# When and where the first expert's weights are split into high and low parts

## The chip, the cores and the metric

The kernel runs on one core of a Trainium2 chip. The metric is the device time of one execution in microseconds (us), as the median of several runs. Five engines work at once, each through its own queue in the order of the program: TensorE (PE, matrix products; its weight loads show as PEld), VectorE (DVE), ScalarE (ACT), GpSimd (POOL) and SyncE (SP), which issues most transfers. ScalarE and GpSimd issue some too.

## The reference

Three stages follow one another, on 4 x 448 = 1792 tokens of width 768:

```python
scores = scale * q @ k.T                 # 4 batches, 12 heads, 448 x 448
scores = einsum('bhij,hg->bgij', scores, w_pre)
attn = softmax(scores)
attn = einsum('bhij,hg->bgij', attn, w_post)
x = attn @ v                             # as 1792 x 768
...
expert_idx = argmax(normalised(x) @ normalised(expert_emb).T / tau)
out[mask] = gate[mask] * (relu(x[mask] @ w1[e]) @ w2[e])   # 8 experts, 768 -> 1024 -> 768
...
h = x @ w_in                             # 768 -> 2048 -> 768
g = h - tanh(h)
return g @ w_out
```

## The kernel before

**Precision.** Weights and activations come as 32-bit floats, and a product is made of three products of rounded parts: high times high, high times low, low times high. A weight tile is therefore split in two steps: a copy that rounds to the high part, and a subtraction of the high part from the tile, which gives the low part. `split1` (L633) does both: the copy by `cpy` (ScalarE unless told otherwise, L637), the subtraction by `eng` (VectorE unless told otherwise, L639).

**Attention.** The score rows are cut into blocks of ten rows times twelve heads. The loop at L1013 goes over the steps s; in step s the block s is multiplied by `w_pre` on TensorE (`emit_P`, tile `P`), VectorE takes its row maximum, and ScalarE its exponential with the row sum (L374). In the next step VectorE makes the scaled weights `w` from `wpost` and the row sums (`emit_W`, L384). Two steps after its start the block is multiplied by `w` on TensorE (`T_mm`, tile `T`, L406) and ScalarE copies the result to `A` (L411). Side work has a position in the table `side`: `at(pos, fn, ...)` puts a call into step pos. `emit_AV` multiplies `A` by v, `emit_X` transposes that to token rows, writes them to `x_d` in memory and makes the routing logits, and `emit_R` assigns tokens to experts, in five parts.

**The way to the experts.** `to_experts` in step NBK - 7 opens the buffers of the expert stage and requests four tiles of w1 and four of w2 (`feed1`, `feed2`). The weights w1 of an expert are six tiles of 128 x 1024 (chunks c = 0 to 5, 512 KB each). The list `q1` holds all w1 tiles of all experts in order, and each `feed1` requests the next one into a ring of four buffers (`r1`, NB1 = 4); SyncE waits until the buffer's last reader, a subtraction, is through. `do1` splits one tile and then, unless `feed=False`, calls `feed1`. So the number of tiles that are requested and not yet split stays what it is when the first expert starts. Four `do1` calls of expert 0 stand in the steps NBK - 5 to NBK - 2, with the copy on VectorE and the subtraction on GpSimd. After the loop come the chunks 4 and 5 (copy on ScalarE, subtraction on GpSimd, no `feed1`), the last token tiles (`emit_AV`, `emit_X`, `emit_R` with copies on VectorE), the gathers of expert 0's token rows by GpSimd, their transposition (`xsplit`, L654, tiles `xti`, `xhi`, `xli`), and two `feed1` on ScalarE's queue.

**The experts.** For each of eight experts and one overflow item, `h_chunk` makes eight hidden chunks on TensorE (the h phase) while w2 is split by `do2`; some of the chunks also carry a `conv_step`, which loads a piece of a dense weight (`craw`, L107) and stores its conversion (L121). Then `y_half` makes four halves of the output (the y phase), and a list `todo` is interleaved with them: six `do1` for the next expert, three after the first half and three after the second, then its four `xsplit`. The results are copied from PSUM (tile `yi`) by VectorE for the first half of a pair (L675) and by ScalarE for the second (L673). PSUM tiles of `y_half` and `xsplit` share a ring of five buffers.

Of the kernel before, what the change touches and what calls it, by code (L numbers as in the profile page):

```python
# [8 lines left out]
F32 = mybir.dt.float32  # L9
F32R = mybir.dt.float32r  # L10
# [20 lines left out]
def body(ctx: ExitStack, tc, q, k, v, w_pre, w_post, emb, tau, w1, w2, win, wout, out):  # L31
    nc = tc.nc
    pe, act, dve, pool, sp = nc.tensor, nc.scalar, nc.vector, nc.gpsimd, nc.sync
# [3 lines left out]
    E, _, FF = w1.shape  # L37
# [3 lines left out]
    KD = DM // 128  # L41
# [83 lines left out]
    if True:  # L125
# [209 lines left out]
        for T in range(4 * B):  # L335
            n = IT[T % 4][1]
# [6 lines left out]
        NBK = len(blocks)  # L343
# [19 lines left out]
        def emit_P(i):  # L363
            n = 12 * blocks[i][2]
            t = sr.pop(i)
            pt = ps("b", f"P{i}")
            pe.matmul(pt[:n, :S], wpre[:n, :n], t[:n, :], start=True, stop=True)  # L367

            flush2()
            mx = a2.tile([120, 4], F32, tag="mx", name=f"mx{i}", bufs=5)  # L370
            dve.tensor_reduce(mx[:n, 0:1], pt[:n, :S], op=ALU.max, axis=AX.X, negate=True)  # L371
            p = a2.tile([120, S], F32, tag="p", name=f"p{i}", bufs=LAG + 1)
            pj[i] = (p, mx)
            return lambda: act.activation(p[:n, :], pt[:n, :S], AF.Exp, bias=mx[:n, 0:1], scale=1.0, accum_out=mx[:n, 1:2])  # L374
# [3 lines left out]
        def emit_W(i):  # L378
            n = 12 * blocks[i][2]
            p, mx = pj[i]  # L380
            dve.tensor_scalar_add(mx[:n, 2:3], mx[:n, 1:2], 1e-9)  # L381
            dve.reciprocal(mx[:n, 3:4], mx[:n, 2:3])
            w = a2.tile([120, 120], F32, tag="w", name=f"w{i}", bufs=3)
            dve.tensor_scalar_mul(w[:n, :], wpost[:n, :], mx[:n, 3:4])  # L384
            wj[i] = w
# [4 lines left out]
        def emit_T(i):  # L390
            T, r, m = blocks[i]
            n = 12 * m
            b, it = divmod(T, 4)
            if r == 0:
                A[T] = aA.tile([CP, NJ, H, 120], F32, tag="A", name=f"A{T}", bufs=2)
            p, mx = pj.pop(i)
            w = wj.pop(i)
            wv = w.rearrange("p (g i) -> p g i", i=10)[:n, :, :m]
            pt = ps("c", f"T{i}")
            pv = pt[:CP, :NJ * n].rearrange("p (c g i) -> p c g i", c=NJ, i=m)  # L400
            tev[i] = (pt, pv, p, w, wv, n, m)

        def T_mm(i, c0, c1):
            pt, pv, p, w, wv, n, m = tev[i]
            for c in range(c0, c1):
                pe.matmul(pt[:CP, c * n:(c + 1) * n] if m == 10 else pv[:, c], p[:n, c * CP:(c + 1) * CP], w[:n, :] if m == 10 else wv,  # L406
                          start=True, stop=True)

        def emit_TE(i):
            T, r, m = blocks[i]  # L410
            act.copy(A[T][:, :, :, 10 * r:10 * r + m], tev.pop(i)[1])  # L411
# [202 lines left out]
    with mctx:  # L614
        mp, mq = [None], [None]
# [17 lines left out]
        def split1(t, tag, nm, n, eng=dve, cpy=act.copy):  # L633
            w = t.shape[1]
            pl = mp[0] if tag == "w1" else mq[0]
            hi = pl.tile([128, w], F32R, tag=tag + "h", name=f"{tag}h{nm}", bufs=n)
            cpy(hi, t)  # L637
            lo = pl.tile([128, w], F32R, tag=tag + "l", name=f"{tag}l{nm}", bufs=n)
            eng.tensor_sub(lo, t, hi.bitcast(F32))  # L639
            return hi, lo  # L640

        def gather(idx, nm):
            t = mp[0].tile([128, DM], F32, tag="xg", name=f"xg{nm}", bufs=3)
            pool.indirect_dma_start(out=t, out_offset=None, in_=x_d, in_offset=bass.IndirectOffsetOnAxis(ap=idx, axis=0))
            return t

        def xtile(nm):
            return tuple(mq[0].tile([128, KD, 256], F32R, tag=tg, name=f"{tg}{nm}") for tg in ("xh", "xl"))
# [166 lines left out]
        def src1(e, c):  # L815
            return osrc[0](c) if e == OV else w1[e, c * 128:(c + 1) * 128, :]
# [7 lines left out]
        r1, r2 = {}, {}  # L824

        def feed1(eng=sp):
            if q1:
                n, e, c = q1.pop()
                r1[n, c] = mp[0].tile([128, FF], F32, tag="r1", name=f"r1_{n}_{c}", bufs=NB1)
                eng.dma_start(r1[n, c], src1(e, c))  # L830

        def feed2():
            if q2:
                n, e, f = q2.pop()
                r2[n, f] = mp[0].tile([128, DM], F32, tag="r2", name=f"r2_{n}_{f}", bufs=NB2)
                sp.dma_start(r2[n, f], src2(e, f))

        def do1(n, c, out_, eng=dve, cpy=act.copy, feed=True):
            out_.append(split1(r1.pop((n, c)), "w1", f"i{n}_{c}", KD, eng, cpy))
            if feed:  # L840
                feed1()

        def do2(n, f, out_, eng=dve):
            out_.append(split1(r2.pop((n, f)), "w2", f"i{n}_{f}", KF, eng))
            feed2()

        def gathers(n):
            e = items[n]
            ix = [osrc[2]] if e == OV else [ids[:, 2 * e + j:2 * e + j + 1] for j in range(2)]
            return [gather(i, f"i{n}_{j}") for j, i in enumerate(ix)]  # L850
# [4 lines left out]
        def at(pos, fn, *a):  # L855
            side.setdefault(int(pos), []).append((fn, a))
# [68 lines left out]
        w1c = []  # L925
# [8 lines left out]

        at(NBK - 7, to_experts)
        for c in range(4):
            at(NBK - 5 + c, do1, 0, c, w1c, pool, dve.tensor_copy)

        def relay_to(i):
            while nxt[0] <= min(i, NBK - 1) and blocks[nxt[0]][0] in sdone:  # L940
                emit_relay(nxt[0])
                nxt[0] += 1
# [4 lines left out]
        def flush(tag=None):  # L947
            keep = []
            while late:
                x = late.pop(0)  # L950
                if tag in (None, x[0]):
                    y = x[1]()
                    if x[0] == "e" and callable(y):
                        late2.append((x[0], y))
                else:
                    keep.append(x)
            late.extend(keep)
            if tag:
                flush2(tag)
# [9 lines left out]
        def run_fill(fn, a):  # L969
            tag = "d" if fn is emit_AV2 else "e"  # L970
            if fn is emit_S2:
                flush("d")
                flush("e")
            elif fn is not emit_S:
                flush(tag)
            e = fn(*a)
            if fn in (emit_S, emit_S2):
                e()
                if a[1] + (fn is emit_S2) == NP - 1:
                    sdone.add(a[0])  # L980
            else:
                late.append((tag, e))
# [30 lines left out]
        for s in range(NBK + LAG + 6):  # L1013
            todo = side.get(s, [])
            fill = [x for x in todo if x[0] in PEF]
            for fn, a in todo:
                if fn in (load_q, load_k, load_v, conv_load, zero_fill):
                    fn(*a)
            flush()
            relay_to(s + NSR - 1)  # L1020
            ex = emit_P(s) if s < NBK else lambda: None
            if 0 <= s - 1 < NBK:
                emit_W(s - 1)
            for fn, a in todo:
                if fn is emit_R and a[1] in (0, 1, 3):
                    fn(*a)
            i = s - LAG
            on = 0 <= i < NBK
            fill.sort(key=lambda x: x[0] not in (emit_S, emit_S2, emit_AV2))
            if fill and fill[0][0] in (emit_S, emit_S2, emit_AV2):  # L1030
                run_fill(*fill.pop(0))
            ex()
            for fn, a in todo:
                if fn is conv_do:
                    fn(*a)
            if on:
                emit_T(i)
                T_mm(i, 0, NJ)
                flush("d")
                emit_TE(i)  # L1040
            for x in fill:
                run_fill(*x)
            for fn, a in todo:
                if fn in (to_experts, do1) or fn is emit_R and a[1] in (2, 4):
                    fn(*a)
        flush()
        flush2()
# [2 lines left out]

        ps_late()
        TL = 4 * B - 1
        for c in range(4, KD):
            do1(0, c, w1c, pool, feed=False)
        emit_X(TL - 1, 0)()
        for p in range(3):
            emit_AV(TL, p, dve.tensor_copy)()
# [8 lines left out]
        for x in range(5):  # L1066
            emit_R(len(RG) - 1, x)
        xg = gathers(0)
        xhl = xtile("i0")
        for j, t in enumerate(xg):  # L1070
            for hf in range(2):
# [5 lines left out]
        for n, e in enumerate(items):  # L1077
# [49 lines left out]
            if not last:  # L1127
                w1c, xhl = nw1, nx
# [251 lines left out]
```

## Time and profile before

| What | Before |
|---|---|
| median of 3 runs (lowest to highest) | 1370.86 us (1370.37 to 1372.72) |
| the profiled execution's own time | 1376.32 us |
| its span, first to last instruction | 1374.6 us |
| TensorE busy | 1312.8 us (96%) |
| VectorE busy | 1017.7 us (74%) |
| ScalarE busy | 736.7 us (54%) |
| GpSimd busy | 502.8 us (37%) |
| mean granted TensorE clock | 0.977 of full speed |

The profile shows one execution. All times of the trace count from the span's first instruction. The block loop ends near 518 us, the experts run from 539 to about 845 us, and the dense stage follows. A share of busy time is a mean over stages that differ; what a change in one place is worth is read from the waits of that place.

### The profile page before, as it was taken

The numbers are of one execution on the slowest core, as the hardware profiler recorded it, in microseconds if no ns is written. First come the engines' busy times: TensorE is split into PE (matmuls) and PEld (weight loads), VectorE is DVE, ScalarE is ACT, GpSimd is POOL, SyncE is SP. The second block draws the span as 40 slices with busy tenths as digits, with TensorE's granted clock in tenths as the row PEclk, the third lists the DMA queues.
The fourth block names the chain that finished last, engine by engine and source line by source line (L and its number), as shares of the span: only waits on it lengthen the run. The fifth ranks groups of instructions, "written<-read, shape, count | busy, mean of one in ns | idle before, by whom it ended". The sixth has DMA issues, their size and how long they took to land. (4 is left out here: it accounts for less than half of the span.)

```text
span 1374.6 us, 24956 instructions
## 1 busy us (share of the span) xinstructions
PE 1312.8 (96%) x9104; PEld 1146.0 (83%) x9104; DVE 1017.7 (74%) x2189; ACT 736.7 (54%) x1518; POOL 502.8 (37%) x495
## 2 busy tenths in 40 slices
PE   7999999999999987999999997899999989999998
PEld 5777776776777766999999996699998889999998
DVE  4776787678677773677776764688888788788886
ACT  5666666675666653545444453554444444544441
POOL 0233333333333323333332422544454334444432
PEclk9999999999999997999999999799999999999999
DMA  6886675667556564778877872421113133121102
GB/s 153 247 253 190 185 209 168 170 201 202 160 173 204 164 205 147 263 253 262 273 233 238 254 220 84 136 69 47 46 48 109 37 96 107 67 61 55 47 24 81
DMA packets 149412, 210.90 MB, mean 153 GB/s; under 512 B 54022, under 2 KB 109494, under 8 KB 149286
## 3 DMA queue, kind: packets, MB, share of 16 engines
q1 hardware_dynamic: 145104, 194.19, 46.4%
q0 software_dynamic: 2640, 12.19, 2.8%
q10 hardware_dynamic: 1542, 2.89, 0.7%
q8 instruction: 73, 1.20, 0.4%
q14 instruction: 53, 0.43, 0.1%
HBM read 135.70 MB, written 35.00 MB: 124 GB/s over the span
## 5 line engine op out<-in xcount | busy, mean ns | idle before, releaser
L406 PEld LDWEIGHTS T<-w,p 120*112 120x112 f32 (+1 forms) x1440 | 166.4, 177 | 66.8 <-issue 44.5
L120 POOL TENSOR_TENSOR cm<-cm,ct 128x256 f32<-128x256 f32 x96 | 70.1, 731 | 404.9 <-DVE ct L117 360.9
L406 PE MATMUL T<-w,p 120*112 120x120 f32 (+1 forms) x1440 | 185.6, 272 | 6.2 <-DVE w L384 3.0
L374 ACT ACTIVATE p<-P,mx 120x448 f32<-120x448 f32 x180 | 114.0, 633 | 119.8 <-DVE mx L381 106.3
L1220 POOL TENSOR_TENSOR gl<-th,gh 128x448 fp32r<-128x448 f32 x64 | 74.8, 1169 | 261.0 <-ACT gh L1219 192.6
L367 PE MATMUL P<-sr,wpre 120*120 120x448 f32 x360 | 166.2, 544 | 1.4 <-ACT p L374 1.4
L1271 PE MATMUL o<-woh,gh 128*128 128x384 f32 x448 | 152.5, 340 | 5.3 <-DVE acc L1277 5.3
L1240 ACT ACTIVATE u<-h 128x448 f32<-128x448 f32 x64 | 34.9, 546 | 222.9 <-PE h L1236 219.2
L1272 PE MATMUL o<-wol,gh 128*128 128x384 f32 x448 | 150.7, 336 | 0.0
L1273 PE MATMUL o<-woh,gl 128*128 128x384 f32 x448 | 150.7, 336 | 0.0
L371 DVE TENSOR_REDUCE mx<-P 120x1 f32<-120x448 f32 x180 | 111.4, 619 | 49.4 <-PE P L367 48.6
L1236 PE MATMUL h<-yh,wil 128*128 128x448 f32 x384 | 143.8, 374 | 3.3 <-POOL wil L1209 3.3
L1234 PE MATMUL h<-yh,wih 128*128 128x448 f32 x384 | 144.0, 375 | 1.1 <-ACT wih L1208 0.6
L1277 DVE TENSOR_TENSOR acc<-acc,o 128x384 f32<-128x384 f32 x196 | 106.9, 548 | 51.4 <-PE o L1273 51.4
L1235 PE MATMUL h<-yl,wih 128*128 128x448 f32 x384 | 143.9, 375 | 0.5 <-DVE yl L1183 0.5
L411 ACT COPY A<-T 112x480 f32<-112x480 f32 x180 | 101.5, 564 | 16.2 <-PE T L406 15.6
L686 PE MATMUL hi<-xhi,w1hi 128*128 128x256 f32 x384 | 108.8, 283 | 0.0
L687 PE MATMUL hi<-xli,w1hi 128*128 128x256 f32 x384 | 108.6, 283 | 0.0
L688 PE MATMUL hi<-xhi,w1li 128*128 128x256 f32 x384 | 108.4, 282 | 0.0
L424 PEld LDWEIGHTS AV<-A,v 112*64 112x64 f32 x1536 | 74.8, 138 | 23.9 <-issue 10.5
L669 PE MATMUL ypi<-w2hi,hhi 128*128 128x384 f32 x272 | 93.2, 343 | 0.1
L670 PE MATMUL ypi<-w2li,hhi 128*128 128x384 f32 x272 | 92.1, 338 | 0.6 <-DVE w2li L639 0.3
(223 smaller groups left out, 3279.9 us busy)
## 6 DMA issues: line engine op xcount, KB each, us to landing
sr<-ssb SPq DMA_DIRECT2D x176, 210.0 KB
r<-in_moe_w SPq DMA_DIRECT2D x72, 384.0 KB
r<-in_moe_w SPq DMA_DIRECT2D x52, 512.0 KB
craw<-in_moe_w_in SPq DMA_DIRECT2D x48, 256.0 KB
craw<-in_moe_w_out SPq DMA_DIRECT2D x48, 256.0 KB
raw<-wi_d SPq DMA_DIRECT2D x15, 768.0 KB
wor<-wo_d SPq DMA_DIRECT2D x15, 768.0 KB
wi_d<-cm SPq DMA_DIRECT2D x48, 128.0 KB
```

The costliest lines, as they stand in the source:

```text
L367: pe.matmul(pt[:n, :S], wpre[:n, :n], t[:n, :], start=True, stop=True)
L371: dve.tensor_reduce(mx[:n, 0:1], pt[:n, :S], op=ALU.max, axis=AX.X, negate=True)
L374: return lambda: act.activation(p[:n, :], pt[:n, :S], AF.Exp, bias=mx[:n, 0:1], scale=1.0, accum_out=mx[:n, 1:2])
L406: pe.matmul(pt[:CP, c * n:(c + 1) * n] if m == 10 else pv[:, c], p[:n, c * CP:(c + 1) * CP], w[:n, :] if m == 10 else wv, start=True, stop ...
L686: pe.matmul(pt[:, :256], wh[:, sl], xh[:, c, :], start=c == 0, stop=False)
L687: pe.matmul(pt[:, :256], wh[:, sl], xl[:, c, :], start=False, stop=False)
L1234: pe.matmul(pt[:, :S], wi[0][:, c, sl], yh[:, c, :], start=c == 0, stop=False)
L1235: pe.matmul(pt[:, :S], wi[0][:, c, sl], yl[:, c, :], start=False, stop=False)
L1236: pe.matmul(pt[:, :S], wi[1][:, c, sl], yh[:, c, :], start=False, stop=c == KD - 1)
L1271: pe.matmul(pt[:, :384], gh[:, sl], wo[0][:, f, n0:n0 + 384], start=f == 0, stop=False)
L1272: pe.matmul(pt[:, :384], gh[:, sl], wo[1][:, f, n0:n0 + 384], start=False, stop=False)
L1273: pe.matmul(pt[:, :384], gl[:, sl], wo[0][:, f, n0:n0 + 384], start=False, stop=f == GF - 1)
```

## The change

Two functions take the place of `do1` for the chunks 0 to 3 of the first expert. `do1_hi` makes the high part with a copy on ScalarE, in the steps NBK - 4 to NBK - 1. `do1_lo` makes the low part; the four calls stand behind the loop, two on VectorE (each with a `feed1`) and two on GpSimd (without). The chunks 4 and 5 are split after the last routing step and the gathers, with the subtraction on VectorE in place of GpSimd.

```diff
+        def do1_hi(n, c):
+            t = r1.pop((n, c))
+            hi = mp[0].tile([128, FF], F32R, tag="w1h", name=f"w1hi{n}_{c}", bufs=KD)
+            act.copy(hi, t)
+            early.append((n, c, t, hi))
+
+        def do1_lo(out_, eng, feed):
+            n, c, t, hi = early.pop(0)
+            lo = mp[0].tile([128, FF], F32R, tag="w1l", name=f"w1li{n}_{c}", bufs=KD)
+            eng.tensor_sub(lo, t, hi.bitcast(F32))
+            out_.append((hi, lo))
+            if feed:
+                feed1()
+
+        early = []
...
         for c in range(4):
-            at(NBK - 5 + c, do1, 0, c, w1c, pool, dve.tensor_copy)
+            at(NBK - 4 + c, do1_hi, 0, c)
...
-                if fn in (to_experts, do1) or fn is emit_R and a[1] in (2, 4):
+                if fn in (to_experts, do1_hi) or fn is emit_R and a[1] in (2, 4):
...
         TL = 4 * B - 1
-        for c in range(4, KD):
-            do1(0, c, w1c, pool, feed=False)
+        for c in range(4):
+            do1_lo(w1c, dve if c < 2 else pool, c < 2)
         emit_X(TL - 1, 0)()
...
         xg = gathers(0)
+        for c in range(4, KD):
+            do1(0, c, w1c, dve, feed=False)
         xhl = xtile("i0")
```

## Rows read from the trace of the kernel before

**Rows 1.** The page: TensorE's and the other engines' busy time and share.

```profile
PE 1312.8 (96%) x9104; PEld 1146.0 (83%) x9104; DVE 1017.7 (74%) x2189; ACT 736.7 (54%) x1518; POOL 502.8 (37%) x495
```

**Rows 2.** Stretches: length, busy us of PE, PEld, DVE, ACT, POOL; clock, DMA share, GB/s.

```profile
499.00:516.00 17.00, 12.37 (x117) 9.49 (x116) 15.96 (x42) 6.40 (x17) 9.40 (x4) 0.93 0.78 267
530.00:539.00 9.00, 2.97 (x13) 2.30 (x13) 1.15 (x3) 1.43 (x3) 5.25 (x6) 0.53 0.48 143
513.00:517.00 4.00, 4.00 (x39) 3.69 (x38) 2.58 (x7) 1.50 (x4) 1.77 (x1) 0.57 0.61 181
```

**Rows 3.** Timeline of VectorE in the last blocks: start, duration, line, tiles.

```profile
501.00 0.69 DVE L637 CAST w1hi<-r 128x1024 fp32r<-128x1024 f32 x1
...
502.51 1.74 DVE L384 TENSOR_SCALAR w<-wpost,mx 120x120 f32<-120x120 f32 x1
...
513.16 1.69 DVE L384 TENSOR_SCALAR w<-wpost,mx 120x120 f32<-120x120 f32 x1
...
515.45 0.28 DVE L384 TENSOR_SCALAR w<-wpost,mx 96x120 f32<-96x120 f32 x1
```

**Rows 4.** Timeline of GpSimd in the last blocks, first and last of four.

```profile
501.82 2.36 POOL L639 TENSOR_TENSOR w1li<-r,w1hi 128x1024 fp32r<-128x1024 f32 x1 [23.15 <-DMA r<-in_moe_w]
...
512.41 2.35 POOL L639 TENSOR_TENSOR w1li<-r,w1hi 128x1024 fp32r<-128x1024 f32 x1 [0.76 <-DVE w1hi L637]
```

**Rows 5.** Timeline of ScalarE in an earlier block.

```profile
494.71 0.62 ACT L374 ACTIVATE p<-P,mx 120x448 f32<-120x448 f32 x1
...
495.31 0.56 ACT L411 COPY A<-T 112x480 f32<-112x480 f32 x1
```

**Rows 6.** Timeline of TensorE at the end of the blocks.

```profile
515.66 2.45 PE L406 MATMUL T<-w,p 120*112 120x120 f32 x16
```

**Rows 7.** Timeline of SyncE's queue at the second expert's y phase.

```profile
600.59 0.42 SPq L107 DMA_DIRECT2D craw<-in_moe_w_out  x1
601.29 10.18 SPq L830 DMA_DIRECT2D r<-in_moe_w  x6
```

**Rows 8.** ScalarE: its casts' waits in the expert stage (us, times, longest); one cast.

```profile
ACT w1hi L637 <- DMA r<-in_moe_w: 17.0, 14, 4.2
...
608.81 1.05 ACT L637 CAST w1hi<-r 128x1024 fp32r<-128x1024 f32 x1 [2.59 <-DMA r<-in_moe_w]
```

**Rows 9.** Timeline of VectorE at two boundaries between experts.

```profile
609.89 1.23 DVE L639 TENSOR_TENSOR w1li<-r,w1hi 128x1024 fp32r<-128x1024 f32 x1 [2.41 <-ACT w1hi L637]
611.04 0.55 DVE L675 COPY yi<-ypi 128x384 f32<-128x384 f32 x1
...
757.03 0.55 DVE L675 COPY yi<-ypi 128x384 f32<-128x384 f32 x1
```

**Rows 10.** TensorE's waits in the expert stage (us, times, longest); three of them.

```profile
PE xti L654 <- DVE yi L675: 6.1, 4, 2.7
...
611.64 0.55 PE L654 MATMUL xti<-ident,xgi 128*128 128x128 f32 x3 [1.73 <-DVE yi L675]
...
683.53 0.55 PE L654 MATMUL xti<-ident,xgi 128*128 128x128 f32 x3 [1.19 <-DVE yi L675]
...
721.30 0.55 PE L654 MATMUL xti<-ident,xgi 128*128 128x128 f32 x3 [2.67 <-DVE yi L675]
```

**Rows 11.** Stretches of the expert stage, columns as in rows 2.

```profile
601.00:609.00 8.00, 8.00 (x50) 7.97 (x49) 4.99 (x5) 2.67 (x4) 2.40 (x3) 1.00 0.88 305
716.00:718.00 2.00, 2.00 (x14) 2.00 (x13) 0.00 (x0) 0.85 (x1) 1.49 (x2) 1.00 0.99 399
721.00:727.00 6.00, 5.70 (x30) 5.71 (x31) 2.10 (x5) 0.96 (x2) 0.00 (x0) 0.72 0.70 238
```

**Rows 12.** Timelines of VectorE and GpSimd in the first expert's h phase.

```profile
549.57 1.45 DVE L639 TENSOR_TENSOR w2li<-r,w2hi 128x768 fp32r<-128x768 f32 x1
...
551.50 0.96 DVE L639 TENSOR_TENSOR w2li<-r,w2hi 128x768 fp32r<-128x768 f32 x1
...
549.47 0.73 POOL L120 TENSOR_TENSOR cm<-cm,ct 128x256 f32<-128x256 f32 x1 [10.21 <-DVE ct L117]
```

## The prediction, made before the change was run

> **What bounds the kernel now.** I read the page's engine table first, then the stretches around the edit, then the timeline of each engine in them, and last the waits of the expert stage that follows. TensorE is busy nearly the whole span [rows 1]; an edit gains only where TensorE is idle or slowed, and loses wherever it makes a new gap. Around the edit there is such a place: from 499 to 516 us VectorE is busy 15.96 of 17 us and TensorE only 12.37 [rows 2]. The VectorE timeline shows why: the scaling `w` at L384 takes 0.28 us when it is alone and 1.67 to 1.74 us four times in a row, once in each of the blocks that also carry a weight cast of 0.68 us [rows 3]. GpSimd's subtraction of 2.35 us covers each of them, and each `w` ends within 0.1 us of that subtraction's end (504.25 after 504.18, 514.85 after 514.76) [rows 4]. So these blocks wait for VectorE, and VectorE waits for GpSimd. The last blocks' transposes then run at a granted clock that averages 0.57, partly at the lower level (1.2 GHz), after those gaps [rows 2, 6].
>
> The second place is the expert stage, since the edit also changes what is loaded ahead there. At each boundary between experts a chain ends last: weight load, ScalarE cast, VectorE subtraction, VectorE copy `yi`, then TensorE's transpose `xti`, whose PSUM buffer that copy frees. At 608.81 the sixth cast has waited 2.59 us for its load, its subtraction starts at 609.89, `yi` at 611.04, and TensorE stands still 1.73 us until 611.64 [rows 8 to 10]. Four boundaries show such gaps, 6.1 us in all, and ScalarE's casts waited for loads 14 times, 17.0 us [rows 8, 10].
>
> **Part one, the last blocks: a gain.** Taken off VectorE: four casts of 0.68 (2.7 us) and four prolonged `w` of 1.45 us too much (5.8 us), together 8.5 us, the upper bound of this part. Given back: ScalarE now has per block its exponential (0.62), its copy of `A` (0.56) and the new copy. VectorE's casts become ScalarE copies; the ScalarE form takes 1.05 us [rows 5, 8]. That is 2.2 us a block, some 2.0 with their overlap, where VectorE takes 3.55 from one `w` to the next ((513.16 - 502.51) / 3 [rows 3]). I walk it: the first of the four exponentials can start near 501.7, one step of VectorE after 501.00, where its first cast stood; the third new copy ends near 508.2 and the last block's exponential near 508.7, so its `w` could start at 509.2. But the diff does not hold GpSimd's subtractions back until the last block is through: nothing stands ahead of them in GpSimd's queue, so the one for c = 2 starts at 508.2 and keeps that `w` to about 510.6. This is one stall of the four. VectorE then finishes the blocks at 510.6 instead of 515.73 [rows 3]: 5.1 us. From there to the end of the last transposes took 2.4 us at the lower clock [rows 6]; two groups at full clock need about 1.2, which adds 1.2. VectorE's two new subtractions (1.23 each, priced by the same form in [rows 9]) stand before the tail's small copies, which TensorE needs only some matmuls later; I charge 0.5 us. Gain: 5.1 + 1.2 - 0.5 = 5.8 us, between 2.5 (ScalarE slower, the second GpSimd subtraction also ahead of `w`) and 9.
>
> A rule speaks against spreading the low parts over both engines. The trace: the 768-wide subtraction takes 0.96 us alone and 1.45 us when it starts at 549.57 under a GpSimd operation that runs from 549.47 to 550.20 [rows 12]. The Trainium skill (SBUF — State Buffer, "Who interferes with whom") says that a VectorE instruction with two SBUF inputs and a GpSimd instruction that reads SBUF exclude each other for a whole instruction, and whoever comes first goes first; this trace agrees, with 1.45 against 0.96 us. By the row alone the gain is 5.8 us; by that rule, with both GpSimd subtractions first, 3.4. That is a rival below.
>
> **Part two, chunks 4 and 5 of the first expert: no cost.** Their loads move from 504 us to about 512, when VectorE's subtractions free the buffers; their casts and subtractions move behind the gathers. Between 530 and 539 us, while all wait for the gathered rows, VectorE is busy 1.15 of 9 us and ScalarE 1.43 [rows 2], which covers 2 x 1.05 and 2 x 1.23 us. Without that cover the second pair would delay the first expert by up to 2.5 us. A load asked for at 512 has landed by 520: the one behind the cast at 608.81 was asked for after 601.29 [rows 7, 8].
>
> **Part three, the loads that are no longer issued: a loss.** Before, each of four `do1` calls in the blocks issued a further load, and two more came on ScalarE's queue, so the first expert began with four w1 tiles of the next one requested. After, only c < 2 issue one; with the two from ScalarE's queue the first expert begins with two. Every later `do1` issues exactly one, so the lead stays at two instead of four to the end of the stage. In each y phase, tiles 2 and 3 of the next expert must then be loaded as well as 4 and 5, and before them. SyncE's queue works in order: it comes to these loads after the conversion store and `craw` load at 600.59, just before the first w1 load of that phase at 601.29 [rows 7]. So tile 5 has two tiles more ahead of it. A tile is 524 KB and the queues move 399 GB/s when w1 loads alone fill them [rows 11]: 1.3 us each, 2.6 us, the upper bound. SyncE can issue the first of them 0.3 to 0.9 us sooner, and the queues are 0.88 busy, 1 us idle in 8 [rows 11]; if both helped fully, 1.0 us would stay, the lower bound. The queues are idle mostly before the loads arrive, so I take 2.1 us, nearer the upper end. ScalarE's copy `yi` queues behind the late casts, but its PSUM buffer is wanted only a transpose later, so only the chain named above, through tile 5, counts.
>
> There are seven full boundaries. Four have a gap already, so all 2.1 us is added; the other three have slack between the end of `yi` and the transpose, at the widest 0.8 us (`yi` ends at 757.58 [rows 9]) and 1.1 us in all: 7 x 2.1 - 1.1 = 13.6 us. The eighth, to the overflow item, shows no wait of a cast for its load; I count nothing. Then the clock: after the 2.67 us gap that ends at 721.30 the granted clock fell to the lower level, averaging 0.72 over 6 us, 1.7 us of lost work; after 1.73 and 1.19 us it did not [rows 10, 11]. With 2.1 us more, the gaps of 1.73 and 1.19 become 3.8 and 3.3 us: two further falls, 3.4 us. Loss 13.6 + 3.4 = 17.0 us.
>
> **The sum.** 17.0 - 5.8 = 11.2 us slower. The profiled execution took 1376.32 us, 5.5 us (0.4%) above the median of 1370.86; its sum is 1387.5, and the same 11.2 us on the median gives 1382.1.
>
> **Rivals.** *The loads still land in time* (0.17): the opposite sign. Loads for the expert after next, which now share the queues with tiles 4 and 5, come later in the new order, and if that and the idle share hide the two tiles, only part one stays: 1370.9 - 5.8 = 1365. It decides below 1.0 us of delay a boundary, where 7 x 1.0 - 1.1 equals the gain. Against it stand the 14 waits for loads that exist even with a lead of four. *A wash* (0.12): 0.6 to 1.4 us a boundary and no further fall of the clock, 3.1 to 8.7 us of loss, 1368 to 1374. *The clock falls at every boundary* (0.15): 2.6 us each, 17.1 us, and six further falls, 10.2 us: with the gain 21.5 us slower, 1392. For it: one gap of 2.67 us sufficed. Against it: three boundaries start with slack. *The two engines take turns* (0.11): both GpSimd subtractions ahead of the last `w`, the gain 3.4 us, 1384.5. For it are the four prolonged `w` of now; against it, VectorE is waiting already when the first of them ends. The forecast has 0.45.
>
> **How the numbers follow.** A measurement of this kernel tells about 0.2% (2.7 us) from no change. Slower 0.45 + 0.15 + 0.11 = 0.71, same 0.12, faster 0.17. The likeliest case alone, with 1.6 to 2.6 us a boundary, spans 1378 to 1388. The 8-in-10 range goes on to 1366, leaving out about half of the faster rival, and to 1391, leaving out the end of the clock rival.
>
> **What would show it.** Right: no `w` above 0.3 us but the last one or two; the last transposes 5 to 7 us earlier; ScalarE's casts for c = 2 to 5 of each expert waiting for loads, far above 17 us in total; gaps before `xti` at all seven boundaries, near 20 us instead of 6.1; more stretches at the lower clock. Wrong: if tile 5's cast starts no later after the y phase begins than now, the loss isn't there and the kernel is faster by the gain of part one.

## The result, and the profile after

| What | Before | After |
|---|---|---|
| median (lowest to highest), 4 runs each | 1370.61 us (1369.47 to 1372.72) | 1386.15 us (1386.04 to 1389.15) |
| ratio, with its 95% interval | | 1.0114 (1.0097 to 1.013) |
| the profiled execution: time, span | 1376.32, 1374.6 us | 1386.18, 1384.5 us |
| mean granted TensorE clock | 0.977 | 0.975 |

The kernel is 15.5 us slower; 11.2 were predicted. The profiled executions differ by 9.9 us only, because the one before was a long one, as the last sections show.

**The last blocks.** The page's engine row shows little; the stretch that answers to the first of [rows 2], in the same columns, shows much:

```profile
PE 1314.5 (95%) x9104; PEld 1147.8 (83%) x9104; DVE 1017.8 (74%) x2189; ACT 741.3 (54%) x1522; POOL 500.5 (36%) x491
```

```profile
499.00:516.00 17.00, 16.67 (x214) 14.11 (x214) 11.99 (x40) 11.83 (x25) 6.97 (x2) 1.00 0.57 210
```

TensorE is busy 16.67 of 17 us instead of 12.37, at full clock. The timeline of VectorE shows how:

```profile
506.47 0.28 DVE L384 TENSOR_SCALAR w<-wpost,mx 120x120 f32<-120x120 f32 x1
507.85 1.53 DVE L384 TENSOR_SCALAR w<-wpost,mx 96x120 f32<-96x120 f32 x1
509.31 2.35 DVE L852 TENSOR_TENSOR w1li<-r,w1hi 128x1024 fp32r<-128x1024 f32 x2
522.21 2.35 DVE L639 TENSOR_TENSOR w1li<-r,w1hi 128x1024 fp32r<-128x1024 f32 x2
```

Every `w` takes 0.28 us but the last, where [rows 3] had four long ones. The timelines of GpSimd, ScalarE and TensorE, each in its own order of time:

```profile
506.90 6.97 POOL L852 TENSOR_TENSOR w1li<-r,w1hi 128x1024 fp32r<-128x1024 f32 x2 [29.63 <-ACT w1hi L846]
...
501.39 1.05 ACT L846 CAST w1hi<-r 128x1024 fp32r<-128x1024 f32 x1
...
519.81 1.98 ACT L637 CAST w1hi<-r 128x1024 fp32r<-128x1024 f32 x2
...
508.73 1.85 PE L406 MATMUL T<-w,p 120*112 120x120 f32 x16
...
527.73 1.51 PE L654 MATMUL xti<-ident,xgi 128*128 128x128 f32 x6 [5.87 <-DMA xgi<-x_d,ids]
...
531.45 0.58 PE L686 MATMUL hi<-xhi,w1hi 128*128 128x256 f32 x1
```

GpSimd's first subtraction starts at 506.90, as soon as the third high part is there, and the `w` at 507.85 is the one that meets it. GpSimd's two subtractions then take 6.97 us, where two alone take 4.7 (2 x 2.35, [rows 4]): VectorE's pair stands between them and takes no longer than alone, 2.35 us. Chunks 4 and 5 (519.81 and 522.21) are through before the first gathered rows reach TensorE at 527.73. The first expert's first product starts at 531.45 us, against 538.98 before.

Of these 7.5 us, 1.4 were there already before the edit acts: the 22nd product with `w_pre`, counted back from the last one, starts at 482.81 before and at 481.42 after. From it to the first expert it was 56.17 us and is 50.03: the gain is **6.1 us** (4.9 against a second profile of the kernel before, experiment 4). No run separates what the casts cost VectorE from what GpSimd's subtractions cost it.

**The expert stage.** The waits of the stage (us, times, longest), and four of the seven gaps before `xti`, on TensorE's timeline:

```profile
ACT w1hi L637 <- DMA r<-in_moe_w: 61.9, 26, 8.8
PE xti L654 <- DVE yi L675: 19.4, 7, 4.0
```

```profile
567.61 0.55 PE L654 MATMUL xti<-ident,xgi 128*128 128x128 f32 x3 [2.06 <-DVE yi L675]
608.57 0.55 PE L654 MATMUL xti<-ident,xgi 128*128 128x128 f32 x3 [3.68 <-DVE yi L675]
648.53 0.55 PE L654 MATMUL xti<-ident,xgi 128*128 128x128 f32 x3 [3.32 <-DVE yi L675]
...
726.88 0.90 PE L654 MATMUL xti<-ident,xgi 128*128 128x128 f32 x3 [3.95 <-DVE yi L675]
```

All seven boundaries have a gap; they sum to 19.4 us instead of 6.1 [rows 10]. The queue of SyncE and the casts of ScalarE at the boundary that [rows 7, 8] showed:

```profile
595.58 0.42 SPq L107 DMA_DIRECT2D craw<-in_moe_w_out  x1
596.05 9.83 SPq L830 DMA_DIRECT2D r<-in_moe_w  x6
...
591.99 1.05 ACT L637 CAST w1hi<-r 128x1024 fp32r<-128x1024 f32 x1
600.17 1.05 ACT L637 CAST w1hi<-r 128x1024 fp32r<-128x1024 f32 x1 [7.13 <-DMA r<-in_moe_w]
...
605.74 1.05 ACT L637 CAST w1hi<-r 128x1024 fp32r<-128x1024 f32 x1 [0.21 <-DMA r<-in_moe_w]
```

The first load is requested at 596.05, and the cast of tile 2 waits 7.13 us for it. Here lies the new wait: not in tile 5, which waits 0.21, but in tile 2, behind which the others queue. From the first w1 cast of a y phase to its sixth the mean over the seven phases is 12.2 us before and 14.1 after.

**The clock.** Stretches of the kernel after, columns as in [rows 2], the last of them 5 us from the first expert's first products; under it the same 5 us of the kernel before:

```profile
568.20:571.60 3.40, 3.40 (x12) 3.40 (x11) 1.21 (x3) 0.47 (x1) 0.00 (x0) 0.50 0.66 262
...
725.20:732.00 6.80, 5.12 (x18) 5.12 (x19) 3.57 (x7) 1.59 (x5) 0.00 (x0) 0.50 0.47 150
649.00:655.00 6.00, 6.00 (x47) 6.00 (x47) 2.30 (x5) 2.07 (x4) 0.00 (x0) 1.00 0.66 220
...
531.50:536.50 5.00, 4.99 (x32) 4.70 (x32) 1.58 (x4) 1.59 (x3) 0.55 (x1) 0.74 0.78 268
```

```profile
539.00:544.00 5.00, 4.99 (x22) 4.70 (x22) 1.08 (x2) 0.88 (x3) 0.26 (x1) 0.50 0.81 269
```

Beside four gaps the clock is at the lower level (1.2 GHz): 3.4 us from 568.2, 609.2 and 687.7, and 6.8 us from 725.2. Before there was one such stretch of 3.4 us. TensorE was busy 3 x 3.40 + 5.12 = 15.3 us at half clock, which is 7.7 us of lost work against 1.7: 6.0 us more. The first expert in turn leaves the lower level earlier: (0.74 - 0.50) x 5 = 1.2 us less lost. 13.3 of gaps + 6.0 - 1.2 = 18.1 us; from the first expert's first product to the overflow item's the stage took 309.12 us against 290.92, **18.2 us** more. With 18.2 - 6.1 = 12.1 the change is accounted for; the 1.4 us ahead of the edit and 0.8 in the dense stage take the spans' difference to 9.9.

### The profile page after: what moved, and what is told of

Read it like the earlier page. It is cut to its first block, busy times and chain, and to the rows that moved or that the text cites. A ratio compares the mean times of both kernels' runs of the same rounds, so it can differ in the third digit from the quotient of the medians.

```text
span 1384.5 us, 24927 instructions
## 1 busy us (share of the span) xinstructions
PE 1314.5 (95%) x9104; PEld 1147.8 (83%) x9104; DVE 1017.8 (74%) x2189; ACT 741.3 (54%) x1522; POOL 500.5 (36%) x491
## 5 line engine op out<-in xcount | busy, mean ns | idle before, releaser
L120 POOL TENSOR_TENSOR cm<-cm,ct 128x256 f32<-128x256 f32 x96 | 70.3, 732 | 417.6 <-DVE ct L117 380.5
L411 ACT COPY A<-T 112x480 f32<-112x480 f32 x180 | 101.6, 564 | 15.5 <-PE T L406 15.0
L119 POOL TENSOR_SCALAR cm<-cm 128x256 f32<-128x256 f32 x96 | 92.9, 967 | 8.4
```

## The experiments

The lead, the number of w1 tiles that are requested and not yet split when an expert begins, is set by the `feed1` calls around the first expert. The table gathers what the runs showed; "last blocks" is the time from the same `w_pre` product to the first expert, "gaps" those before `xti`, "casts" their waits for loads, "1st to 6th" the mean from the first to the sixth w1 cast of a y phase. Ratios are to the kernel before in the same set of runs, with 95% intervals.

| Kernel | Ratio | Last blocks, us | Gaps, us (number) | Casts, us (number) | 1st to 6th, us |
|---|---|---|---|---|---|
| before, first profile | 1 | 56.2 | 6.1 (4) | 17.0 (14) | 12.2 |
| before, second profile | 1 | 54.9 | 4.7 (3) | 15.1 (14) | 11.9 |
| after, lead 2 | 1.0114 (1.0097 to 1.013) | 50.0 | 19.4 (7) | 61.9 (26) | 14.1 |
| after with lead 4 | 0.9945 (0.9926 to 0.9963) | 50.4 | 4.8 (4) | 16.9 (14) | 12.2 |
| before with lead 2 | 1.0137 (1.0116 to 1.0158) | 54.5 | 18.4 (7) | 61.2 (25) | 14.0 |
| after with lead 3 | 0.9991 (0.9977 to 1.0005) | 50.0 | 8.2 (6) | 19.2 (21) | 12.6 |
| lead 4, all low parts on VectorE | 0.9946 (0.9929 to 0.9964) | 49.5 | 5.3 (5) | 16.4 (14) | 12.1 |
| lead 4, GpSimd's low parts first | one run, 1370.39 us | 55.8 | 5.7 (4) | 16.3 (14) | 12.1 |
| lead 4, chunks 4 and 5 early | 0.9998 (0.9986 to 1.001) | 52.5 | 4.9 (4) | 16.1 (14) | 12.0 |
| lead 4, four requests moved to the h phase | 1.0018 (1.0004 to 1.0032) | 50.0 | 9.9 (6) | 38.4 (21) | 12.7 |
| lead 2, two requests moved to the h phase | 0.9954 (0.9934 to 0.9974) | 49.6 | 6.0 (5) | 12.7 (11) | 12.2 |
| lead 4, lows on VectorE, `do1` earlier | 0.9979 (0.9967 to 0.9992) | 49.8 | 5.6 (4) | 22.9 (16) | 11.9 |

**1. The change with the lead put back.** Four requests on ScalarE's queue instead of two.

```diff
-        for c in range(4, KD):
+        for c in range(4):
             feed1(act)
```

> The changed kernel, but four w1 tiles instead of two are requested on ScalarE's queue before the first expert, so that four tiles are ahead again. Theory A (the loss is the lost lead): the seven gaps before xti fall from 19.4 us to about 6, and only the gain of the blocks stays: 1362 to 1367 us, against 1370.6 before and 1386.2 with the change. Theory B (the loss comes from the moved split work, whatever is requested ahead): still 1383 to 1389 us. If the two share the loss: about 1375.

The waits of the expert stage:

```profile
ACT w1hi L637 <- DMA r<-in_moe_w: 16.9, 14, 2.9
...
PE xti L654 <- DVE yi L675: 4.8, 4, 2.0
```

Median 1367.53 us, ratio 0.9945: 0.5 us above the range expected, in a set of runs whose kernel before took 1372.64 us. The gaps are back at 4.8 us and the casts' waits at 16.9, while the last blocks keep their gain (50.4 us). So the whole loss hangs on the lead, and the rest of the change makes the kernel faster.

**2. The kernel before with the smaller lead alone.**

```diff
-            at(NBK - 5 + c, do1, 0, c, w1c, pool, dve.tensor_copy)
+            at(NBK - 5 + c, do1, 0, c, w1c, pool, dve.tensor_copy, c < 2)
```

> The kernel before, with the split work where it was, but the do1 calls for c = 2 and 3 in the blocks request no further tile, so that two tiles are ahead. Theory A: 17 to 22 us slower than before, 1388 to 1393 us, with gaps before xti at all seven boundaries. Theory B: 1369 to 1373 us, as before.

Median 1391.0 us, ratio 1.0137, with the last blocks as long as before. The waits, in the columns used above:

```profile
ACT w1hi L637 <- DMA r<-in_moe_w: 61.2, 25, 8.0
...
PE xti L654 <- DVE yi L675: 18.4, 7, 3.6
```

The loss stands alone here, with nothing of the new code. By the ratios the two parts add up: -0.0055 + 0.0137 = +0.0082, of the order of the 0.0114 of the whole change; the intervals leave some 0.003 open. The profiled execution was the fastest of its four, 1385.72 us. Its expert stage took 304.70 us, 15.4 more than experiment 1's 289.35: 13.6 us of gaps and one further clock stretch of 3.4 us at half clock, 1.7 us of work. The other three took 1390.49 to 1395.9 us at a mean granted clock of 0.976 to 0.970, where the profiled one had 0.979.

**3. A lead of three.** `range(3)` in the edit of experiment 1.

> The changed kernel with three tiles requested on ScalarE's queue, so that three are ahead. Theory A with a delay of one tile (1.3 us) a boundary: about half of the loss of the change stays, 1372 to 1378 us. If the lead matters only below a threshold of three: as with four, 1362 to 1367. Theory B: 1383 to 1389 us.

The waits at the gaps:

```profile
PE xti L654 <- DVE yi L675: 8.2, 6, 2.0
```

Median 1371.68 us, ratio 0.9991, gaps 8.2 us: just below the range expected if a tile costs 1.3 us a boundary. The first tile taken from the lead costs 8.2 - 4.8 = 3.4 us of gaps, 0.5 a boundary, and the second 19.4 - 8.2 = 11.2, 1.6 a boundary. The loss is not proportional, but the first tile is not free: the expert stage took 289.35 us with four tiles ahead, 294.87 with three and 309.12 with two, and the intervals of the ratios with four and with three do not meet (0.9945 against 0.9991, some 6 us). The sixth cast comes 0.4 us later in the y phase with three than with four, and 1.6 later again with two. A tile takes 1.3 us of the queues [rows 11]; that the first one partly filled time in which they were idle fits both steps roughly (1.3 - 0.4 = 0.9 us hidden, and of the second nothing), but was not measured by itself.

**4. The kernel before once more.** Unchanged, for a second profile.

> The kernel before, unchanged, for a second profile: the profile shown took 1376.3 us and its median run 1370.6. If a typical execution lacks the fall of the clock after the gap that ends at 721 us, or has smaller gaps in the expert stage, this profile shows it: 1370 to 1372 us, the gaps before xti at most 6 us in all. If the profile itself costs the time, it is 1375 to 1377 again.

1371.69 us, span 1370.0, 4.7 us shorter than the first profile: 1.4 us ahead of the edit, 1.3 in the last blocks, 2.3 in the expert stage, -0.3 behind it. Its gaps were 1.64, 1.07 and 1.98 us, with one clock stretch. The third stretch of [rows 2], in this execution:

```profile
513.00:517.00 4.00, 3.71 (x52) 3.34 (x50) 1.25 (x6) 2.39 (x5) 0.41 (x1) 1.00 0.51 155
```

The fall of the clock to 0.57 at the end of the blocks is not here, nor in experiment 2, which has the same blocks: the last transposes took 1.87 and 1.86 us in them, not 2.45. So that fall belonged to one execution and not to the kernel, and with it the 1.3 us of the last blocks. Against this profile, whose time is within 0.1% of the median, the change costs 20.5 us in the experts and gains 4.9.

**5. All four low parts on VectorE**, with the lead of four.

```diff
-            do1_lo(w1c, dve if c < 2 else pool, c < 2)
+            do1_lo(w1c, dve, c < 2)
```

> The kernel with four tiles ahead, and all four low parts on VectorE behind the loop, none on GpSimd. If GpSimd's subtraction is what prolongs the last block's w (1.52 us with four tiles ahead, 0.28 us alone), that w takes 0.28 us here and the last transposes start about 1.2 us earlier; against that stand 2.4 us more of VectorE work before the tail's copies, hidden while TensorE has matmuls queued. First expert's first matmul 0 to 1 us earlier than with GpSimd, whole kernel 1364 to 1369 us. If the w is late for another reason (ScalarE), it stays at 1.5 us and the tail gets up to 2 us longer.

VectorE's timeline:

```profile
506.98 0.28 DVE L384 TENSOR_SCALAR w<-wpost,mx 96x120 f32<-96x120 f32 x1
507.26 4.63 DVE L852 TENSOR_TENSOR w1li<-r,w1hi 128x1024 fp32r<-128x1024 f32 x4
```

The last `w` takes 0.28 us, 1.25 less than with GpSimd's subtraction under it, and the last blocks are 0.9 us shorter. The four subtractions of 4.63 us in a row delay nothing that shows. The ratio, 0.9946, cannot be told from experiment 1's: 0.9 us is within both intervals. With a median of 1365.04 us (1364.20 to 1366.94) this version beats both kernels.

**6. The engines of the low parts exchanged**, so that GpSimd starts first.

```diff
-            do1_lo(w1c, dve if c < 2 else pool, c < 2)
+            do1_lo(w1c, pool if c < 2 else dve, c < 2)
```

> The kernel with four tiles ahead, with the low parts of c = 0 and 1 on GpSimd and of 2 and 3 on VectorE. GpSimd is not held back by the loop, so its subtractions start after the first and the second new copy, some 4 us earlier. If they keep VectorE from w: two or three w of 1 to 1.7 us instead of one, and the last transposes 1 to 3 us later. If GpSimd's subtraction is harmless inside the blocks: every w at 0.28 us and the last transposes earlier.

Timelines of GpSimd, VectorE and TensorE:

```profile
501.58 4.71 POOL L852 TENSOR_TENSOR w1li<-r,w1hi 128x1024 fp32r<-128x1024 f32 x2 [25.26 <-ACT w1hi L846]
...
501.58 4.86 DVE L525 TENSOR_SCALAR p<-iota_s,posk 128x256 f16<-128x256 f32 x2
...
510.21 0.28 DVE L384 TENSOR_SCALAR w<-wpost,mx 96x120 f32<-96x120 f32 x1
...
506.49 0.20 PE L533 MATMUL M<-oht,p 128*128 128x8 f16 x2 [1.88 <-DVE p L525]
...
508.29 1.94 PE L406 MATMUL T<-w,p 120*112 120x120 f32 x8 [1.60 <-ACT A L411]
```

```profile
507.60:514.40 6.80, 6.11 (x44) 5.58 (x45) 4.29 (x11) 4.06 (x9) 0.00 (x0) 0.50 0.17 67
```

The line by itself is a stretch, columns as in [rows 2]. I had looked at the wrong victim: every `w` stayed at 0.28 us. A pair of routing operations at L525 takes 4.86 us instead of 0.62, from the start of GpSimd's pair to 0.15 us after its end, and no `w` stood under it; TensorE stands still 1.88 and 1.60 us, then runs 6.8 us at the lower clock level. The last blocks take 55.8 us: the gain is gone. That is the price of GpSimd's work under VectorE's in these blocks, 5.4 us for two subtractions, and it is what the change avoids by asking GpSimd late. Not every VectorE instruction is held so. In the kernel before, the two small ones of `emit_W` ahead of `w` keep their length under GpSimd's subtraction from 501.82 to 504.18 [rows 4]: a reciprocal of 0.16 us at 502.31, and this one:

```profile
502.13 0.14 DVE L381 TENSOR_SCALAR mx<-mx 120x1 f32<-120x1 f32 x1
```

**7. Chunks 4 and 5 ahead of the last token tiles**, on GpSimd as before the change, with the lead of four.

```diff
+        for c in range(4, KD):
+            do1(0, c, w1c, pool, feed=False)
         emit_X(TL - 1, 0)()
...
-        for c in range(4, KD):
-            do1(0, c, w1c, dve, feed=False)
```

> The kernel with four tiles ahead, and chunks 4 and 5 split right behind the four low parts, on ScalarE and GpSimd as before the change, instead of behind the gathers. Their loads are now requested only when VectorE's subtractions are through, near 511 us, and land near 515 to 517. ScalarE then waits for them ahead of the tail's copies: the first expert starts 4 to 6 us later, 1368 to 1373 us. If the place of these two chunks costs nothing either way, as before the change, it starts within 1 us of the kernel with four ahead.

ScalarE's timeline, then TensorE's:

```profile
513.56 1.04 ACT L637 CAST w1hi<-r 128x1024 fp32r<-128x1024 f32 x1 [3.04 <-DMA r<-in_moe_w]
...
516.50 0.83 PE L424 MATMUL AV<-A,v 112*64 112x88 f32 x16 [2.92 <-DVE lg L463]
```

ScalarE waits 3.04 us for a load in front of the copies that the token tiles need, and TensorE stands still 2.92 us at 516.50. The last blocks take 52.5 us, 2.1 more than in experiment 1, where 4 to 6 were expected. The median is 1371.06 us, ratio 0.9998, so the move of these two chunks behind the gathers belongs to the gain. The profiled execution was the fastest of this kernel's, 1365.9 us, so 2.1 us is what the profile shows, and the remainder of the 7 us between the ratios (0.0053 x 1371) is not placed. The nine other executions, 1368.37 to 1373.03 us, have a mean granted clock of 0.977 to 0.981, the profiled one 0.982; where they lost it no trace shows.

**8. Lead of four, four of the six requests in the h phase.** To tell whether the requests that follow (for the expert after next) are what slows tiles 4 and 5.

```diff
+                    if n and f in (2, 3, 5, 6):
+                        feed1()
...
-                todo = [lambda c=c: do1(n + 1, c, nw1) for c in range(KD)]
+                todo = [lambda c=c: do1(n + 1, c, nw1, feed=c < 2) for c in range(KD)]
```

> The kernel with four tiles ahead, but in the y phase only tiles 4 and 5 of the next expert are requested; the four tiles of the expert after that are requested one by one in the next h phase. If those four, queued behind tiles 4 and 5, slow them, the gaps before xti fall from 4.8 us to under 3 and the casts' waits from 16.9 us to under 10: 1361 to 1366 us. If the queues serve loads in order, so that later requests cost tiles 4 and 5 nothing, gaps and waits stay as with four ahead: 1364 to 1369 us. If the h phase has no room for them, tiles 2 and 3 come late and it is slower than 1370 us.

Ratio 1.0018; gaps 9.9 us, casts' waits 38.4 us, 21 times. At the second boundary the cast of tile 2, now requested at the sixth of the eight hidden chunks, waited 2.96 us, and that of tile 4, requested early in the y phase and with one request behind it, 4.41 us. Here tiles 2 and 3 are late themselves, so this boundary does not tell what the later requests do; the third case of the expectation came true. The first boundary does tell: there tiles 0 to 3 are requested as in experiment 1 and only the later requests are missing. The casts of tiles 4 and 5 waited 1.10 and 0.20 us at it, 1.37 and 0.23 in experiment 1, so the later requests cost at most 0.3 us. That points to the time of a tile's own request, which experiment 9 tries.

**9. The change as it is, with two requests of each expert moved ahead into the h phase.** The lead at the start of each expert stays two.

```diff
+                    if f < 2:
+                        feed1()
...
-                todo = [lambda c=c: do1(n + 1, c, nw1) for c in range(KD)]
+                todo = [lambda c=c: do1(n + 1, c, nw1, feed=c < 4) for c in range(KD)]
```

> The changed kernel with two tiles ahead in the y phase as it is, but two more requested at the start of each h phase (after the first and second do2) and none after the last two do1 of the y phase. So the number requested by the y phase is four again, tiles 2 and 3 have an h phase of 17 us to arrive, and tiles 4 and 5 are alone ahead of the next expert's first two. Theory A (tiles 2 and 3 standing ahead of 4 and 5 in the y phase is the loss): gaps before xti 4 to 6 us, casts' waits 15 to 20 us, 1363 to 1369 us. If instead any load in the h phase comes late there, as with four of them: gaps 8 to 11 us, 1370 to 1376. If the changed kernel's loss has another cause: 1383 to 1389.

The waits:

```profile
ACT w1hi L637 <- DMA r<-in_moe_w: 12.7, 11, 3.1
...
PE xti L654 <- DVE yi L675: 6.0, 5, 2.2
```

Median 1366.86 us, ratio 0.9954: the loss is cured without touching the first expert. What counts is not how many tiles are requested when the expert begins, but how early tiles 2 and 3 are. SyncE's queue ahead of the second expert's y phase, whose first w1 cast starts at 587.05 us here and at 589.25 in experiment 8; first the two requests of this experiment, then those of tiles 2 and 3 in experiment 8:

```profile
572.53 0.38 SPq L830 DMA_DIRECT2D r<-in_moe_w  x1
575.00 0.42 SPq L830 DMA_DIRECT2D r<-in_moe_w  x1
...
586.99 0.43 SPq L830 DMA_DIRECT2D r<-in_moe_w  x1
589.76 0.86 SPq L830 DMA_DIRECT2D r<-in_moe_w  x1
```

Requested 12 us and more ahead of the y phase, tiles 2 and 3 wait for nothing. Experiment 8 has three of the four requested when its y phase begins and the fourth 0.5 us later, and tile 2 is 2.96 us late: a request has to go out well before the phase, not only before its tile is wanted.

**10. The first two `do1` of each y phase ahead of it**, on the kernel of experiment 5, to have SyncE's requests earlier still.

```diff
+            for fn in todo[:2]:
+                fn()
+            todo = todo[2:]
             for ci, col in enumerate(cols):
```

> The kernel with four tiles ahead and all low parts on VectorE, and in the expert stage the first two do1 of the next expert stand before the first y half instead of behind it. Their subtractions then don't queue behind the copy yi, which waits for that half, and free the buffers for tiles 4 and 5 about 2 us sooner. If the late request of tiles 4 and 5 makes the remaining gaps: 5.3 us of gaps fall to under 1.5, casts' waits to under 10 us, 1358 to 1363 us. If SyncE comes to these requests no sooner, held by the conversion's store before them: gaps stay at 4 to 6 us, 1364 to 1368.

VectorE's timeline, then those of GpSimd and of SyncE's queue:

```profile
592.84 2.90 DVE L639 TENSOR_TENSOR w1li<-r,w1hi 128x1024 fp32r<-128x1024 f32 x2
595.67 0.55 DVE L675 COPY yi<-ypi 128x384 f32<-128x384 f32 x1
...
593.08 1.59 POOL L120 TENSOR_TENSOR cm<-cm,ct 128x256 f32<-128x256 f32 x1 [4.84 <-DVE ct L117]
...
594.69 0.33 SPq L121 DMA_DIRECT2D wo_d<-cm  x1
595.07 0.42 SPq L107 DMA_DIRECT2D craw<-in_moe_w_out  x1
595.59 9.92 SPq L830 DMA_DIRECT2D r<-in_moe_w  x6
```

The subtractions now stand ahead of `yi`, but SyncE comes to the first w1 load only at 595.59, 0.52 us after the `craw` load before it (0.70 in [rows 7]). The conversion's store at 594.69 stands ahead in its queue, and it waits for GpSimd's `cm` (L120), which ends at 594.66. That operation takes 1.59 us where it took 0.74 in experiment 5: VectorE's two subtractions now overlap it, so the new order itself held the store back by 0.85 us. The gaps stay (5.6 against 5.3 us), the median of 1368.37 us is 0.4 above the range expected, and the ratio is 0.0033 above experiment 5's, in another set of runs. At this boundary the requests are not limited by when a buffer is free, but by what SyncE does first.

## Why the prediction was right

**The bound and the two places** were right. TensorE lost time where VectorE waited for GpSimd, and at the boundaries of the experts.

**Part one** was sized right, in part by luck: 6.1 us in the profiles it was made from, against 5.8 (4.9 against the second profile). Its term of 1.2 us for the clock came from a fall that the second profile of the kernel before and experiment 2 do not have. The walk had one `w` of four still under a GpSimd subtraction; there is one. It had VectorE through at 510.6; it was at 509.38, or 510.8 when the 1.4 us from ahead of the edit are put back. GpSimd's subtraction for c = 2 started at 506.90 and the last `w` at 507.85; with the same 1.4 us they are at 508.3 and 509.2, as the walk had them (508.2 and 509.2). The two groups of transposes took 1.85 us at full clock, not 1.2, so full clock gave back 0.6 us against the first profile and nothing against the second; and VectorE's two subtractions, charged with 0.5 us, delayed nothing that shows.

**Part two**, nothing, was right, and the cover is needed: experiment 7, which goes without it, starts the first expert 2.1 us later.

**Part three** had the right place, and the right size of its first term: 13.6 us of gaps predicted, 13.3 measured, from a sixth cast that comes 1.9 us later in the y phase (2.2 against the second profile; 2.1 predicted). Experiments 1 and 2 show that the lead alone does it, 8 and 9 that it is how early a tile's own request goes out. The reason for the 2.1 was only partly right: I priced two tiles of 1.3 us less some idle time of the queues spread over both. Experiment 3 shows that the first tile costs 0.5 us of gap a boundary and the second 1.6. My way of counting would have priced a lead of three at about half of the loss; it is 5.5 of 19.8 us of the expert stage.

**The clock** is the term that was mis-sized: "two further falls, 3.4 us". There were three, one of them twice as long, 6.0 us of work, and my rule for them (a gap as long as 2.67 us) failed: see below. The first expert's earlier return to full clock, 1.2 us, I had not counted.

**The sum** was 17.0 - 5.8 = 11.2 us; the profile gives 18.2 - 6.1 = 12.1, and the measured medians 15.5. The rest lies in the base, not in the change: the profiled execution before was itself 4.7 us longer than the second in its span, 2.3 of it in the expert stage and 1.3 in the last blocks. Against the second profile the terms are 14.7 of gaps instead of 13.6, 20.5 in all for the experts, and 4.9 of gain: 15.6 us, less 1.1 in the dense stage, 14.5 of span where the medians differ by 15.5. The likeliest case was put at 1378 to 1388 us; its own terms, 1.6 to 2.6 us a boundary, two falls and the gain, added to the median give 1378.6 to 1385.6, so the measured 1386.15 lies just above what they cover.

**The rivals.** That the loads land in time fell: the casts for tile 2 waited 7 to 9 us. A wash fell with it; at a lead of three it would have been right (0.9991). That the clock falls at every boundary came half true, four of seven. That the two engines take turns is half true as well: they did, but VectorE's pair went between GpSimd's two subtractions, so only one of these lay ahead of the last `w`. The Trainium skill (SBUF — State Buffer, "Who interferes with whom") has whoever comes first go first for a whole instruction. This trace agrees that the two exclude each other, with 6.97 us for GpSimd's pair around VectorE's 2.35 us, and 4.71 where it ran first, in experiment 6. It does not bear out the order: GpSimd's second subtraction started at 509.26 and took 4.61 us, while VectorE's second started later, at 510.44, and was through in its usual 1.21 us. What the rule did not make me see is that the victim can be another VectorE instruction of the block than `w`: the routing's in experiment 6.

What stays open: why the queues hide most of one tile and nothing of the second, which instruction goes first when VectorE and GpSimd meet, and whether a ring of more than four buffers would give more, which was not tried.

## What to carry to other kernels

A call that also requests the next load keeps a pipeline's lead; whoever moves or replaces such calls counts the requests that are left, since a lead that is lost once, in the first expert, stays lost in every later one. Price a lead tile by tile, and look for the point where the loads cease to be hidden: here the first tile taken away cost 5.5 us of the expert stage and the second 14.3. A count of requests is not enough, either: the same four help only if the last of them go out long enough before they are wanted. Where a change has two parts, run each alone: here one was worth -0.55% and the other +1.4%, and the better version has the first without the second.

## What the runs showed of the hardware

- The clock does not follow a gap's length. Beside gaps of 2.06, 3.68, 2.65 and 3.95 us (the falls at 568.2, 609.2, 687.7 and 725.2) the granted clock was at the lower level for 3.4, 3.4, 3.4 and 6.8 us; after one of 3.32 us it stayed at 1.00 (649 to 655 us). Experiment 2, with 18.4 us of gaps at the same seven boundaries, had two such stretches of 3.4 us only. Nor is the number of falls fixed for a kernel: the first profile of the kernel before had one at 513.5 us that the second had not, and experiment 2's four executions had a mean granted clock from 0.979 (1385.72 us) down to 0.970 (1395.9 us).
- A GpSimd subtraction over SBUF prolongs some VectorE instructions that meet it and not others: one of them `w` from 0.28 to 1.53 us, two a pair of routing operations from 0.62 to 4.86 us. In the kernel before, a reciprocal of 0.16 us and a scaling of one column of 0.14 us (502.31 and 502.13) kept their length under it. What tells them apart was not tested. VectorE's pair of subtractions prolongs GpSimd's in turn, from 4.71 to 6.97 us, and is not prolonged itself (2.35 us); in experiment 10 it prolongs GpSimd's `cm` from 0.74 to 1.59 us.
- Two executions of the same kernel differed by 4.7 us of span: 1.4 us ahead of the last blocks, 1.3 with a fall of the clock in them, 2.3 in the expert stage. A sum that is made against one profile carries that.
